# PSUM instead of SBUF for the operands of the small VectorE chain that orders the experts

## The chip, the cores and the metric

The kernel runs on one core of a Trainium2 chip. The metric is the device time of one execution in microseconds; the median of three executions of the kernel before is 777.16 us (775.65 to 778.07). One execution was also taken by the hardware profiler: it lasted 776.65 us, of which the span from the first to the last instruction is 774.9 us. "TensorE" is PE in the rows, with PEld for its weight loads; VectorE is DVE, ScalarE is ACT, GpSimd is POOL, SyncE is SP.

## The reference

Three stages follow each other: linear attention with random features, a top-1 mixture of experts, and a dense MLP.

```python
def phi(x):                                   # attention, per batch and head
    proj = np.einsum('bhsd,md->bhsm', x, omega)
    h = proj - np.sum(x * x, axis=-1, keepdims=True) / 2.0
    return np.exp(h - np.max(h, axis=-1, keepdims=True)) / np.sqrt(m)
num = phi(q_s) @ (phi(k_s).T @ v);  x = num / (den + 1e-06)

logits = x @ w_gate                           # mixture of experts, N = 2304 tokens, D = 512
expert_idx = np.argmax(logits, axis=1)
for e in range(8):                            # F = 1024
    out[mask_e] = gate_w[mask_e] * (relu(x[mask_e] @ w1[e]) @ w2[e])

h = x @ w_in                                  # MLP, d_ff = 2048
g = np.where(h >= 1, h, np.where(h <= -1, 0.0, (h + 1) ** 2 / 4))
return g @ w_out
```

## The kernel before

The attention stage writes the tokens' vectors `x` to a DRAM buffer `xd` and, beside that, finds each token's expert. An order of its instructions is made by a planner (class `Plan`); its tasks use eight PSUM buffers `ps` of 2 KB per partition, which come from a pool `psp` that is closed when the stage ends. The planner's last tasks count the tokens per expert and put the token numbers into lists (`slots`).

After the planner's tasks stands a chain written out by hand in program order (L1061 to L1122). One small TensorE product (L1080) adds up the tokens per expert into PSUM buffer 0. VectorE then copies the eight counts to SBUF (L1082), makes keys from them (L1083, L1084), compares the keys with each other (L1085), sums the comparisons into places (L1086), turns the places into an 8 by 8 one-hot table `hot` (L1088), and uses this table to reorder the counts, the expert numbers, the offsets and the lists (L1089 to L1104). With the offsets per expert, `offe`, L1115 and the six steps after it give each token its position in the ordered output. Every step is one VectorE instruction on at most 144 elements per partition.

Then the expert stage begins. Its tiles of tokens are gathered from `xd` by indirect DMAs that GpSimd issues (L1177), three for each expert. The first three are those of expert 0, whose list is ready before the chain (L935). Four new PSUM pools, `ps_x`, `ps_h`, `ps_y` and `ps_q` (L1158 to L1161, eight buffers of 2 KB per partition), take the room that `psp` had. The first work of the new stage on TensorE is `m_x0`: it runs 14 products whose result nobody reads, into a buffer of `ps_h`, then four transposes of the first gathered tile into buffers of `ps_x` and `ps_y`, then twice three idle products and four transposes:

```python
idle = ps_h.tile([P, 512], F32, name="ph", tag="ph")...          # L1206
for i, _ in rows(0):
    for _ in range((14, 3, 3)[i]):
        nc.tensor.matmul(idle, lhsT=oneb, rhs=oneb..., start=True, stop=True)   # L1209
    for d in range(4):
        m_turn(0, d, i, px[d])                                    # L1183
for d in range(4):
    m_split(0, d, px[d])                                          # L1189, L1190
```

ScalarE and VectorE split the transposed tiles in two parts (L1189, L1190), and TensorE's products of expert 0 follow (L1230 to L1232). The order on each engine is the order of the program, and each engine runs its instructions strictly in that order. A first write into a buffer of a new pool waits until the last instruction that uses the room of the closed pool is done. The offsets `offe` are read by L1115 through this statement, which the change leaves as it is:

```python
nc.vector.tensor_tensor(out=rr, in0=ohall, in1=offe.rearrange("p e o -> p o e").to_broadcast([P, NTILE, E]), op=ALU.mult)
```

Of the kernel before, what the change touches and what calls it, by code (L numbers as in the profile page):

```python
# [14 lines left out]
ALU = mybir.AluOpType  # L15
AX = mybir.AxisListType.X
# [3 lines left out]
P = 128  # L20
B, H, S, HD = 4, 8, 576, 64
NT, D, E, F, FF = 2304, 512, 8, 1024, 2048
NTILE = NT // P
WS = (288, 264, 272, 280, 288, 304, 328, 344)
W = max(WS)
NB = 3
# [10 lines left out]
C_TRI, C_IOTA, C_C8, C_WS, C_THR, C_TOK, C_ID, C_END = 0, 128, 512, 520, 528, 544, 580, 708  # L37
# [174 lines left out]
def kernel(  # L212
# [14 lines left out]
    nc = tc.nc  # L227
# [18 lines left out]
    oneb = cp.tile([P, P], BF16, name="oneb")  # L246
# [3 lines left out]
    rsb, ohall = seen[:, :, 0], seen[:, 0:NTILE, 1]  # L250
# [230 lines left out]
    with ExitStack() as actx:  # L481
# [4 lines left out]
        def ring(n, shape, name, dtype=F32, pool=ac):  # L486
            return [pool.tile(shape, dtype, name=f"{name}{i}") for i in range(n)]

        plan = Plan({
            "ps": ring(8, [P, 4, P], "ps", pool=psp),  # L490
            "blk": ring(7, [P, 2 * H, HD], "blk"),
            "sqt": ring(2, [P, 2 * H, HD], "sqt"),
            "th": ring(4, [P, 4, P], "th"),
            "pp": ring(11, [P, H, P], "pp"),
            "qt": ring(4, [P, 4, P], "qt"),
            "nx": ring(5, [P, H, HZ + 1], "nx"),
            "xr": ring(3, [P, H, HD], "xr"),
# [79 lines left out]
        dve, act, pool = nc.vector, nc.scalar, nc.gpsimd  # L577
# [434 lines left out]
        for s, u in enumerate(units):  # L1012
# [11 lines left out]
            if which == "k" and blk[0] != "s" and blk[1] == 1:  # L1024
                b = blk[0]
# [9 lines left out]
            for us, b0, b1 in new:  # L1035
                t = len(cts)
                kvs = [d for b in {b0, b1} for hf_ in range(2) for d in kvdone[b, hf_]]
                cts.append(c_tasks(t, us, kvs, s + 2 + 0.5 * len(new)))
                if t in groups:
                    t0, n = groups[t]  # L1040
                    prev_run = r_tasks(t0, cts[t0:t0 + n], s + 3.5, prev_run)
            if s >= 4 and s % 6 == 1 and wk < 4:
                key = wseq[wk]
# [5 lines left out]
            if s in (33, 35):  # L1049
                key = wseq[wk]  # L1050
# [10 lines left out]
        def small(name, shape):  # L1061
            return ap.tile(shape, F32, name=name, tag=name, bufs=1)

        def col(c, n):
            return cs[:, c:c + n]

        n, key, at_, nums, off, offe = [small(f"t{i}", [P, E, 1]) for i in range(6)]
        inc, ones, nv = [small(f"u{i}", [P, E]) for i in range(3)]
        hot, prod = small("hot", [P, E, E]), small("prod", [P, NB, E, E])
        g = prod[:, 0:2].rearrange("p m a b -> p (m a b)").rearrange("p (e j) -> p e j", j=16)  # L1070
        tot = small("ttot", [P, 1])

        def row(t):
            return t.rearrange("p a o -> p o a").to_broadcast([P, E, E])

        def flat(t):
            return t[:, :, 0]

        pn = plan.tiles["ps"][0][:, 0, :]
        nc.tensor.matmul(pn[:, 0:E], lhsT=oneb, rhs=rsb[:, NTILE, :], start=True, stop=True)  # L1080
        dve.memset(ones, 1.0)
        dve.tensor_copy(flat(n), pn[:, 0:E])  # L1082
        dve.scalar_tensor_tensor(out=flat(key), in0=flat(n), scalar=8.0, in1=col(C_C8, E), op0=ALU.mult, op1=ALU.add)  # L1083
        dve.memset(key[:, 0, :], 0.0)  # L1084
        dve.tensor_tensor(out=prod[:, 0], in0=row(key), in1=key.to_broadcast([P, E, E]), op=ALU.is_lt)  # L1085
        dve.reduce_sum(flat(at_), prod[:, 0], axis=AX)  # L1086
        iota = col(C_IOTA, E).rearrange("p (e o) -> p e o", o=1)
        dve.tensor_tensor(out=hot, in0=iota.to_broadcast([P, E, E]), in1=row(at_), op=ALU.is_equal)  # L1088
        dve.tensor_tensor(out=prod[:, 0], in0=hot, in1=row(n), op=ALU.mult)  # L1089
        dve.tensor_tensor(out=prod[:, 1], in0=hot, in1=row(iota), op=ALU.mult)  # L1090
        dve.reduce_sum(flat(nums), prod[:, 0], axis=AX)
        dve.reduce_sum(inc, prod[:, 1], axis=AX)
        dve.tensor_copy(ints[:, 4, :], inc)
        dve.tensor_tensor_scan(out=inc, data0=ones, data1=flat(nums), initial=0.0, op0=ALU.mult, op1=ALU.add)
        dve.tensor_sub(flat(off), inc, flat(nums))
        dve.tensor_copy(ints[:, 0, :], flat(off))
# [3 lines left out]
        for m in range(NB):  # L1100
            dve.reduce_sum(slots[:, m, :], prod[:, m], axis=AX)
        dve.tensor_copy(gidx[:, :, 1:E], slots[:, :, 1:E])
        dve.tensor_tensor(out=prod[:, 0], in0=hot.rearrange("p r e -> p e r"), in1=row(off), op=ALU.mult)
        dve.reduce_sum(flat(offe), prod[:, 0], axis=AX)  # L1104
        dve.tensor_sub(flat(n), flat(nums), col(C_WS, E))
        thr = col(C_THR, 16).rearrange("p (o j) -> p o j", o=1).to_broadcast([P, E, 16])
# [13 lines left out]
                                op0=ALU.logical_shift_right)  # L1120
# [495 lines left out]
    for qd in range(1, 4):  # L1616
        if qd == 3:
            z_fetch(2 * ORDER[0])
        for n, p in enumerate(ORDER):
# [11 lines left out]
            if (qd, n) == (3, 2):  # L1631
                flat = yp.tile([P, 3 * YW], F32, name="yF", tag="yT")
# [24 lines left out]
    with tc.If(tot > 0):  # L1657
# [3 lines left out]
        for e in range(E):  # L1661
# [4 lines left out]
            with tc.For_i(0, cnt_e, 1) as i:  # L1666
# [3 lines left out]
                for j in range(16):  # L1670
# [4 lines left out]
                    out=fx, out_offset=None, in_=xd,  # L1675
# [5 lines left out]
                for f in range(8):  # L1681
                    ph = ps_h2.tile([P, 512], F32, name="ph2", tag="ph2")[:, 0:P]
                    o = f % 2 * P
                    for d in range(4):
                        nc.tensor.matmul(ph, lhsT=fw[f // 2 * 4 + d][:, o:o + P],
                                         rhs=fxt[:, d * P:(d + 1) * P], start=(d == 0), stop=(d == 3))
                    nc.vector.tensor_scalar_max(fh[:, f, :], ph, 0.0)
                for j in range(16):
                    c, f = divmod(j, 8)
                    src = w2[ee, f * P:(f + 1) * P, c * 256:(c + 1) * 256]  # L1690
                    nc.sync.dma_start(out=fw[j], in_=src.rearrange("o p f -> p (o f)"))
                for d in range(4):
                    py = ps_h2.tile([P, 512], F32, name="ph2", tag="ph2")[:, 0:P]
                    o = d % 2 * P
                    for f in range(8):
                        nc.tensor.matmul(py, lhsT=fw[d // 2 * 8 + f][:, o:o + P], rhs=fh[:, f, :],
                                         start=(f == 0), stop=(f == 7))
                    nc.scalar.activation(fy[:, d, :], py, AF.Copy)
                po = ps_o.tile([P, D], F32, name="po", tag="po")
                for qd in range(4):  # L1700
# [3 lines left out]
                    for f in range(4):  # L1704
                        ph = ps_h2.tile([P, 512], F32, name="ph2", tag="ph2")[:, 0:P]
                        for d in range(4):
                            nc.tensor.matmul(ph, lhsT=fin[d][:, f * P:(f + 1) * P], rhs=fy[:, d, :],
                                             start=(d == 0), stop=(d == 3))
                        nc.vector.tensor_scalar(out=fg[:, f, :], in0=ph, scalar1=-1.0, scalar2=1.0,
                                                op0=ALU.max, op1=ALU.min)  # L1710
                        nc.scalar.activation(fg[:, f, :], fg[:, f, :], AF.Square, scale=0.5, bias=half)
                        nc.vector.tensor_tensor(out=fg[:, f, :], in0=ph, in1=fg[:, f, :], op=ALU.max)
                    for c in range(4):
# [3 lines left out]
                                         stop=(qd == 3 and c == 3))  # L1717
                nc.vector.tensor_copy(fo, po)
                nc.gpsimd.indirect_dma_start(
                    out=out, out_offset=bass.IndirectOffsetOnAxis(ap=fu, axis=0), in_=fo, in_offset=None)  # L1720
# [36 lines left out]
```

## Time and profile before

| | |
|---|---|
| median of three executions | 777.16 us (775.65 to 778.07) |
| profiled execution | 776.65 us, span 774.9 us |
| TensorE (PE) busy | 745.1 us, 96% of the span |
| PE weight loads (PEld) | 684.0 us, 88% |
| VectorE (DVE) busy | 515.7 us, 67% |
| ScalarE (ACT) busy | 436.7 us, 56% |
| GpSimd (POOL) busy | 376.6 us, 49% |
| mean granted TensorE clock | 0.991 |
| DMA | 164.25 MB, mean 212 GB/s |

A row of the timeline has the start in us from the beginning of the span, the duration in us, the engine, the line, the operation, the tiles by name and the shapes, and in square brackets how long the engine had been idle and what ended that. The chain that is changed lies between 151 and 158 us, at the border between the attention stage and the expert stage.

### The profile page before, as it was taken

The numbers are of one execution on the slowest core, as the hardware profiler recorded it, in microseconds if no ns is written. First come the engines' busy times: TensorE is split into PE (matmuls) and PEld (weight loads), VectorE is DVE, ScalarE is ACT, GpSimd is POOL, SyncE is SP. The second block draws the span as 40 slices with busy tenths as digits, with TensorE's granted clock in tenths as the row PEclk, the third lists the DMA queues.
The fourth block names the chain that finished last, engine by engine and source line by source line (L and its number), as shares of the span: only waits on it lengthen the run. The fifth ranks groups of instructions, "written<-read, shape, count | busy, mean of one in ns | idle before, by whom it ended". The sixth has DMA issues, their size and how long they took to land. (4 is left out here: it accounts for less than half of the span.)

```text
span 774.9 us, 17116 instructions
## 1 busy us (share of the span) xinstructions
PE 745.1 (96%) x6476; PEld 684.0 (88%) x6476; DVE 515.7 (67%) x1104; ACT 436.7 (56%) x1061; POOL 376.6 (49%) x429
## 2 busy tenths in 40 slices
PE   5799999699999999999999999899999999999997
PEld 4698899489999999999988889788998899889985
DVE  3688888965667567565686775876656766575553
ACT  5999999353322222222477766676577655763441
POOL 6665951645654564425548875323343143343212
PEclk9999999899999999999999999999999999999999
DMA  9949511356765765655537769798696996977822
GB/s 231 230 100 255 158 69 30 123 166 179 213 193 178 221 212 179 207 166 161 163 117 305 274 249 330 285 328 269 177 375 189 307 319 168 332 239 285 315 97 85
DMA packets 94236, 164.25 MB, mean 212 GB/s; under 512 B 28528, under 2 KB 61424, under 8 KB 94144
## 3 DMA queue, kind: packets, MB, share of 16 engines
q1 hardware_dynamic: 79680, 94.96, 39.2%
q0 software_dynamic: 14112, 67.44, 27.0%
q8 instruction: 53, 0.87, 0.4%
q10 hardware_dynamic: 352, 0.66, 0.3%
q14 instruction: 39, 0.32, 0.1%
HBM read 122.93 MB, written 40.11 MB: 210 GB/s over the span
## 5 line engine op out<-in xcount | busy, mean ns | idle before, releaser
L1433 PE MATMUL po<-wh,g 128*128 128x512 f32 x288 | 113.8, 395 | 0.7 <-ACT st L1439 0.7
L1435 PE MATMUL po<-wh,g 128*128 128x512 f32 x288 | 113.9, 395 | 0.0
L1434 PE MATMUL po<-wl,g 128*128 128x512 f32 x288 | 113.6, 395 | 0.0
L351 POOL TENSOR_TENSOR wl<-wz,wh 128x256 fp32r<-128x256 f32 (+1 forms) x43 | 40.5, 948 | 95.3 <-ACT wh L365 92.8
L674 ACT ACTIVATE pp<-ps,bi 128x128 f32<-128x128 f32 x288 | 84.4, 487 | 0.0
L329 POOL TENSOR_SCALAR wh<-wra 128x1024 fp32r<-128x1024 f32 x43 | 50.2, 1170 | 61.2 <-DMA wra<-in_moe_w_dram 26.9
L1248 PE MATMUL py<-hh,wh 128*128 128x288 f32 (+6 forms) x256 | 77.5, 303 | 0.0
L1230 PE MATMUL ph<-xh,wh 128*128 128x288 f32 (+6 forms) x256 | 76.7, 300 | 0.7 <-ACT xh L1189 0.4
L1231 PE MATMUL ph<-xl,wh 128*128 128x288 f32 (+6 forms) x256 | 76.6, 299 | 0.1
L1250 PE MATMUL py<-hh,wl 128*128 128x288 f32 (+6 forms) x256 | 76.6, 299 | 0.0
L1232 PE MATMUL ph<-xh,wl 128*128 128x288 f32 (+6 forms) x256 | 76.5, 299 | 0.0
L1249 PE MATMUL py<-hl,wh 128*128 128x288 f32 (+6 forms) x256 | 76.3, 298 | 0.0
L1395 DVE TENSOR_TENSOR g<-cl,g 128x384 fp32r<-128x384 f32 x78 | 47.0, 603 | 38.9 <-ACT g L1391 37.9
L1235 ACT ACTIVATE hh<-ph 128x288 fp32r<-128x288 f32 (+6 forms) x64 | 26.7, 418 | 70.2 <-PE ph L1232 69.1
L1435 PEld LDWEIGHTS po<-wh,g 128*128 128x128 f32 x288 | 54.2, 188 | 13.1 <-DVE g L1395 0.4
L1433 PEld LDWEIGHTS po<-wh,g 128*128 128x128 f32 x288 | 54.2, 188 | 12.4 <-ACT st L1439 1.0
L1434 PEld LDWEIGHTS po<-wl,g 128*128 128x128 f32 x288 | 54.2, 188 | 11.5
L1236 DVE SCALAR_TENSOR_TENSOR hl<-ph,hh 128x288 fp32r<-128x288 f32 (+6 forms) x64 | 29.3, 461 | 52.0 <-ACT hh L1235 51.7
L1391 ACT ACTIVATE g<-cl 128x384 fp32r<-128x384 f32 x78 | 40.5, 520 | 39.7 <-DVE cl L1390 38.4
L441 DVE TENSOR_TENSOR wl<-wra,wh 128x1024 fp32r<-128x1024 f32 x43 | 61.0, 1421 | 2.4 <-POOL wh L329 2.4
L1253 ACT ACTIVATE yT<-py 128x288 f32<-128x288 f32 (+7 forms) x32 | 13.4, 418 | 83.6 <-PE py L1250 80.5
L663 DVE TENSOR_REDUCE nsq<-ps 128x4 f32<-128x512 f32 x72 | 48.1, 683 | 8.1 <-PE ps L658 8.0
(226 smaller groups left out, 2149.8 us busy)
## 6 DMA issues: line engine op xcount, KB each, us to landing
yS<-yd POOLq DMA_DIRECT2D x32, 768.0 KB, 12.2
wra<-in_moe_w_dram SPq DMA_DIRECT2D x43, 512.0 KB, 4.1
ys<-yd POOLq DMA_DIRECT2D x25, 768.0 KB, 11.9
wraw<-in_moe_w_dram SPq DMA_DIRECT2D x20, 512.0 KB, 4.0
yd<-tt SPq DMA_DIRECT2D x24, 384.0 KB, 2.7
yd<-ys SPq DMA_DIRECT2D x9, 768.0 KB, 4.3
wra<-in_moe_w_in_dram SPq DMA_DIRECT2D x12, 512.0 KB, 5.4
wra<-in_moe_w_out_dram SPq DMA_DIRECT2D x11, 512.0 KB, 7.6
```

Source lines behind the costliest of these rows:

```text
L329: nc.gpsimd.tensor_scalar(out=hi, in0=t, scalar1=1.0, scalar2=1.0, op0=ALU.mult, op1=ALU.mult)
L441: nc.vector.tensor_sub(lo, t, hi.bitcast(F32))
L674: act.activation(at(ppb)[:, 2 * j + i, :], at(pjb[i])[:, j, :], AF.Exp, bias=r["bi"][:, j, i:i + 1])
L1230: nc.tensor.matmul(ph, lhsT=wh[:, d, c], rhs=xh, start=(d == 0), stop=False)
L1231: nc.tensor.matmul(ph, lhsT=wh[:, d, c], rhs=xl, start=False, stop=False)
L1232: nc.tensor.matmul(ph, lhsT=wl[:, d, c], rhs=xh, start=False, stop=(d == 3))
L1248: nc.tensor.matmul(py, lhsT=wh[:, a, c], rhs=hh, start=(f == 0), stop=False)
L1249: nc.tensor.matmul(py, lhsT=wh[:, a, c], rhs=hl, start=False, stop=False)
L1250: nc.tensor.matmul(py, lhsT=wl[:, a, c], rhs=hh, start=False, stop=(f == 7))
L1433: nc.tensor.matmul(po, lhsT=gh[:, c], rhs=wh, start=(f == 0), stop=False)
L1434: nc.tensor.matmul(po, lhsT=gh[:, c], rhs=wl, start=False, stop=False)
L1435: nc.tensor.matmul(po, lhsT=gl[:, c], rhs=wh, start=False, stop=(f == 3))
```

## The change

The counts stay in PSUM (`sums`), and the keys (`key`), the places (`at_`), the one-hot table (`hot`) and the offsets per expert (`offe`) are placed in PSUM buffer 0 of the old pool, `plan.tiles["ps"][0]`. The first key is set to zero by a multiplication instead of a memset, and the keys and the counts are copied to SBUF tiles (`keys`, `n`) for the steps that take them as the second input.

```diff
-        n, key, at_, nums, off, offe = [small(f"t{i}", [P, E, 1]) for i in range(6)]
+        pn = plan.tiles["ps"][0]
+        sums, key, at_ = [pn[:, 0, 16 * i:16 * i + E] for i in range(3)]
+        hot = pn[:, 1, 0:E * E].rearrange("p (a b) -> p a b", a=E)
+        nums, off, n, keys = [small(f"t{i}", [P, E, 1]) for i in range(4)]
+        offe = pn[:, 3, 0:E].rearrange("p (e o) -> p e o", o=1)
-        pn = plan.tiles["ps"][0][:, 0, :]
-        nc.tensor.matmul(pn[:, 0:E], lhsT=oneb, rhs=rsb[:, NTILE, :], start=True, stop=True)
-        dve.memset(ones, 1.0)
-        dve.tensor_copy(flat(n), pn[:, 0:E])
-        dve.scalar_tensor_tensor(out=flat(key), in0=flat(n), scalar=8.0, in1=col(C_C8, E), op0=ALU.mult, op1=ALU.add)
-        dve.memset(key[:, 0, :], 0.0)
-        dve.tensor_tensor(out=prod[:, 0], in0=row(key), in1=key.to_broadcast([P, E, E]), op=ALU.is_lt)
-        dve.reduce_sum(flat(at_), prod[:, 0], axis=AX)
-        dve.tensor_tensor(out=hot, in0=iota.to_broadcast([P, E, E]), in1=row(at_), op=ALU.is_equal)
+        nc.tensor.matmul(sums, lhsT=oneb, rhs=rsb[:, NTILE, :], start=True, stop=True)
+        dve.scalar_tensor_tensor(out=key, in0=sums, scalar=8.0, in1=col(C_C8, E), op0=ALU.mult, op1=ALU.add)
+        dve.tensor_scalar(out=key[:, 0:1], in0=key[:, 0:1], scalar1=0.0, scalar2=None, op0=ALU.mult)
+        dve.tensor_copy(flat(keys), key)
+        dve.tensor_copy(flat(n), sums)
+        dve.tensor_tensor(out=prod[:, 0], in0=line(key), in1=keys.to_broadcast([P, E, E]), op=ALU.is_lt)
+        dve.reduce_sum(at_, prod[:, 0], axis=AX)
+        dve.tensor_tensor(out=hot, in0=column(col(C_IOTA, E)), in1=line(at_), op=ALU.is_equal)
         ...
         dve.tensor_copy(ints[:, 4, :], inc)
+        dve.memset(ones, 1.0)
         dve.tensor_tensor_scan(out=inc, data0=ones, data1=flat(nums), initial=0.0, op0=ALU.mult, op1=ALU.add)
         ...
-        dve.tensor_tensor(out=prod[:, 0], in0=hot.rearrange("p r e -> p e r"), in1=row(off), op=ALU.mult)
+        dve.tensor_tensor(out=prod[:, 0], in0=hot.rearrange("p r e -> p e r"), in1=line(flat(off)),
+                          op=ALU.mult)
         dve.reduce_sum(flat(offe), prod[:, 0], axis=AX)
```

VectorE at the beginning of the chain, before (`ps0` is PSUM buffer 0 of the old pool, `t` and `u` are small SBUF tiles; the bracket names the engine whose signal is waited for):

```order
L1081 MEMSET u1_3063 128x8
L1082 COPY t0_3056<-ps0_134 128x8 [waits PE_49]
L1083 SCALAR_TENSOR_TENSOR t1_3057<-t0_3056,cs_95 128x8 [waits DVE_49]
L1084 MEMSET t1_3057 128x1 [waits DVE_49]
L1085 TENSOR_TENSOR prod_3066<-t1_3057 128x64 [waits DVE_49]
L1086 TENSOR_REDUCE t2_3058<-prod_3066 128x8 [waits DVE_49]
```

and VectorE at the same place in the changed kernel:

```order
L1087 SCALAR_TENSOR_TENSOR ps0_134<-ps0_134,cs_95 128x8 [waits PE_49]
L1088 TENSOR_SCALAR ps0_134<-ps0_134 128x1 [waits DVE_49]
L1089 COPY t3_3059<-ps0_134 128x8 [waits DVE_49]
L1090 COPY t2_3058<-ps0_134 128x8
L1091 TENSOR_TENSOR prod_3063<-ps0_134,t3_3059 128x64 [waits DVE_49]
L1092 TENSOR_REDUCE ps0_134<-prod_3063 128x8 [waits DVE_49]
```

The copy out of PSUM is no longer the first step, there is one instruction more ahead of the comparison, and the memset of the ones has moved further down, to stand ahead of the scan.

VectorE near the end of the chain, before (`trr` is written by L1115):

```order
L1103 TENSOR_TENSOR prod_3066<-hot_3065,t4_3060 128x64
L1104 TENSOR_REDUCE t5_3061<-prod_3066 128x8 [waits DVE_49]
L1105 TENSOR_TENSOR t0_3056<-t3_3059,cs_95 128x8
L1107 TENSOR_TENSOR prod_3066<-cs_95,t0_3056 128x128 [waits DVE_49]
L1111 CAST ints_109<-ttot_3067 128x1 [waits DVE_49]
L1115 TENSOR_TENSOR trr_3100<-seen_102,t5_3061 128x144
```

and in the changed kernel:

```order
L1109 TENSOR_TENSOR prod_3063<-ps0_134,t1_3057 128x64
L1111 TENSOR_REDUCE ps0_134<-prod_3063 128x8 [waits DVE_49]
L1112 TENSOR_TENSOR t2_3058<-t0_3056,cs_95 128x8
L1114 TENSOR_TENSOR prod_3063<-cs_95,t2_3058 128x128 [waits DVE_49]
L1118 CAST ints_109<-ttot_3064 128x1 [waits DVE_49]
L1122 TENSOR_TENSOR trr_3097<-seen_102,ps0_134 128x144
```

The instructions stand in the same order, but PSUM buffer 0 is now used until L1122, which is L1115 of the kernel before; before, its last use was L1082.

TensorE at the border of the two stages, before (`ob` and `oa` belong to the last list product, `ph` is the idle products' buffer):

```order
L926 MATMUL ps_136<-oa,ob 128x8
L1080 LDWEIGHTS oneb
L1080 MATMUL ps_134<-seen,oneb 128x8
L1209 LDWEIGHTS oneb [waits DVE_49]
L1209 MATMUL ph<-oneb 128x512 [waits Activation_49]
```

and in the changed kernel:

```order
L926 MATMUL ps_136<-oa,ob 128x8
L1086 LDWEIGHTS oneb
L1086 MATMUL ps_134<-seen,oneb 128x8
L1216 LDWEIGHTS oneb [waits DVE_49,PE_49]
L1216 MATMUL ph<-oneb 128x512 [waits Activation_49]
```

The order on TensorE is the same; at the first idle product a wait for TensorE's own count has been added, and the wait for VectorE stands in the same place. Which of VectorE's instructions fulfils it is not in these rows: in the program before it is L1082, in the changed one L1122. From L1086 on the changed kernel's lines are higher by 6 or 7, so that its L1190 is L1183 of before and its L1216 is L1209.

## Rows read from the trace of the kernel before

**Rows 1.** The page, share of the span by engine:

```profile
PE 745.1 (96%) x6476; PEld 684.0 (88%) x6476; DVE 515.7 (67%) x1104; ACT 436.7 (56%) x1061; POOL 376.6 (49%) x429
```

**Rows 2.** Busy time by stretch: stretch, length, engines, granted clock, DMA share, GB/s:

```profile
159.10:200.00 40.90, 40.55 (x312) 39.91 (x313) 27.01 (x40) 19.61 (x44) 18.78 (x16) 1.00 0.57 173
200.00:250.00 50.00, 50.00 (x414) 49.90 (x414) 31.25 (x42) 11.74 (x31) 28.58 (x22) 1.00 0.66 201
```

**Rows 3.** What TensorE waited for from 159 us to the end:

```profile
PE ph L1540 <- DMA yS<-yd: 1.7, 2, 1.2
PE po L1433 <- ACT st L1439: 0.7, 1, 0.7
PE ph L1405 <- POOL ys L1152: 0.7, 1, 0.7
PE ph L1540 <- ACT tt L1550: 0.5, 1, 0.5
```

**Rows 4.** Timeline of TensorE, 150 to 160 us:

```profile
151.32 4.50 PE L1209 MATMUL ph<-oneb 128*128 128x512 bf16 x14 [0.53 <-DVE t L1082]
155.69 0.41 PE L1183 MATMUL px<-ident,xg 128*128 128x128 f32 x2
...
156.16 0.81 PE L1209 MATMUL ph<-oneb 128*128 128x512 bf16 x3
157.03 0.44 PE L1183 MATMUL px<-ident,xg 128*128 128x128 f32 x2
...
157.52 0.81 PE L1209 MATMUL ph<-oneb 128*128 128x512 bf16 x3
158.26 0.31 PE L1183 MATMUL px<-ident,xg 32*128 32x32 f32 x2
...
159.13 0.40 PE L1230 MATMUL ph<-xh,wh 128*128 128x288 f32 x1 [0.44 <-ACT xh L1189]
```

**Rows 5.** Timeline of VectorE, 149 to 160 us:

```profile
151.11 0.15 DVE L1082 COPY t<-ps 128x8 f32<-128x8 f32 x1
...
151.63 0.22 DVE L1085 TENSOR_TENSOR prod<-t 128x64 f32<-128x64 f32 x1
...
152.40 0.22 DVE L1089 TENSOR_TENSOR prod<-hot,t 128x64 f32<-128x64 f32 x1
...
153.46 0.17 DVE L1095 TENSOR_TENSOR t<-u,t 128x8 f32<-128x8 f32 x1
153.66 0.17 DVE L1096 CAST ints<-t 128x8 int32<-128x8 f32 x1
153.74 0.16 DVE L1097 CAST ints<-t 128x8 int32<-128x8 f32 x1
...
156.41 0.30 DVE L1115 TENSOR_TENSOR trr<-seen,t 128x144 f32<-128x144 bf16 x1
```

**Rows 6.** Timeline of all engines, VectorE just ahead of the chain:

```profile
148.78 0.16 DVE L901 TENSOR_TENSOR rpr<-ps,seen 128x16 f32<-128x16 f32 x1
...
149.06 0.17 DVE L906 TENSOR_REDUCE ps<-rpr 128x2 f32<-128x16 f32 x1
...
149.27 1.02 DVE L918 TENSOR_TENSOR ob<-cs,ps 128x384 bf16<-128x384 f32 x2
```

**Rows 7.** Timeline of GpSimd, 150 to 175 us:

```profile
151.93 1.18 POOL L1177 DMA_INDIRECT xg<-xd,gidx  x1 [2.92 <-DVE prod L1085]
...
158.38 0.95 POOL L1177 DMA_INDIRECT xg<-xd,gidx  x1 [0.31 <-PE ph L1209]
```

**Rows 8.** The idle products' line: count, duration in ns (min/median/max):

```profile
L1209 PE MATMUL ph<-oneb x20: 379/380/635, 151.3 to 158.0; 128*128 128x512 bf16 x20
```

**Rows 9.** Busy time by short stretches, columns as in rows 2:

```profile
150.90:151.30 0.40, 0.00 (x0) 0.00 (x0) 0.33 (x4) 0.00 (x0) 0.00 (x0) 0.50 0.00 0
...
153.50:154.00 0.50, 0.50 (x3) 0.22 (x2) 0.47 (x5) 0.00 (x0) 0.50 (x1) 0.50 0.44 82
154.00:154.50 0.50, 0.50 (x4) 0.20 (x3) 0.50 (x6) 0.00 (x0) 0.38 (x1) 1.00 0.65 180
```

More of the change, by code (lines that the diff above doesn't have):

```diff
@@ L1065, in col @@
             return cs[:, c:c + n]
-        n, key, at_, nums, off, offe = [small(f"t{i}", [P, E, 1]) for i in range(6)]
+        pn = plan.tiles["ps"][0]
[3 more added lines that the diff above has]
+        offe = pn[:, 3, 0:E].rearrange("p (e o) -> p e o", o=1)
         inc, ones, nv = [small(f"u{i}", [P, E]) for i in range(3)]
-        hot, prod = small("hot", [P, E, E]), small("prod", [P, NB, E, E])
+        prod = small("prod", [P, NB, E, E])
@@ L1070, with column, line @@
         g = prod[:, 0:2].rearrange("p m a b -> p (m a b)").rearrange("p (e j) -> p e j", j=16)
         tot = small("ttot", [P, 1])
-        def row(t):
-            return t.rearrange("p a o -> p o a").to_broadcast([P, E, E])
+        def column(t):
+            return t.rearrange("p (e o) -> p e o", o=1).to_broadcast([P, E, E])
+        def line(t):
+            return t.rearrange("p (o e) -> p o e", o=1).to_broadcast([P, E, E])
         def flat(t):
             return t[:, :, 0]
-        pn = plan.tiles["ps"][0][:, 0, :]
@@ L1080 @@
-        nc.tensor.matmul(pn[:, 0:E], lhsT=oneb, rhs=rsb[:, NTILE, :], start=True, stop=True)
-        dve.memset(ones, 1.0)
-        dve.tensor_copy(flat(n), pn[:, 0:E])
-        dve.scalar_tensor_tensor(out=flat(key), in0=flat(n), scalar=8.0, in1=col(C_C8, E), op0=ALU.mult, op1=ALU.add)
-        dve.memset(key[:, 0, :], 0.0)
-        dve.tensor_tensor(out=prod[:, 0], in0=row(key), in1=key.to_broadcast([P, E, E]), op=ALU.is_lt)
-        dve.reduce_sum(flat(at_), prod[:, 0], axis=AX)
-        iota = col(C_IOTA, E).rearrange("p (e o) -> p e o", o=1)
@@ L1088 @@
-        dve.tensor_tensor(out=hot, in0=iota.to_broadcast([P, E, E]), in1=row(at_), op=ALU.is_equal)
-        dve.tensor_tensor(out=prod[:, 0], in0=hot, in1=row(n), op=ALU.mult)
-        dve.tensor_tensor(out=prod[:, 1], in0=hot, in1=row(iota), op=ALU.mult)
+        nc.tensor.matmul(sums, lhsT=oneb, rhs=rsb[:, NTILE, :], start=True, stop=True)
+        dve.scalar_tensor_tensor(out=key, in0=sums, scalar=8.0, in1=col(C_C8, E), op0=ALU.mult, op1=ALU.add)
+        dve.tensor_scalar(out=key[:, 0:1], in0=key[:, 0:1], scalar1=0.0, scalar2=None, op0=ALU.mult)
@@ new lines @@
+        dve.tensor_copy(flat(keys), key)
[3 more added lines that the diff above has]
+        dve.tensor_tensor(out=hot, in0=column(col(C_IOTA, E)), in1=line(at_), op=ALU.is_equal)
+        dve.tensor_tensor(out=prod[:, 0], in0=hot, in1=line(flat(n)), op=ALU.mult)
+        dve.tensor_tensor(out=prod[:, 1], in0=hot, in1=line(col(C_IOTA, E)), op=ALU.mult)
```

## The prediction

> **What bounds the kernel.** I read the shares by engine first: TensorE is busy for 745.1 of 774.9 us [rows 1]. The busy time by stretch says where: from 159.1 us, when the expert stage's products begin, TensorE is busy for 40.55 of 40.90 us and then for 50.00 of 50.00 [rows 2]. The table of its waits from there to the end holds 1.7 + 0.7 + 0.7 + 0.5 = 3.6 us beside the 0.44 us ahead of the first product [rows 3, 4]. So after 159 us the kernel is a row of products with almost no gaps, and whatever sets the moment at which that row begins, sets the end. The chain that the change touches lies just ahead of this moment, so I read the border, 150 to 160 us, engine by engine.
>
> TensorE's part of the border [rows 4]: 14 idle products from 151.32, four transposes from 155.69, three idle products from 156.16, four transposes from 157.03, three idle products, four transposes from 158.26, and the first real product at 159.13. The first idle product was released by L1082, VectorE's copy of the counts, which ends at 151.11 + 0.15 = 151.26 [rows 5]; 0.06 us later TensorE starts. It is the last instruction on VectorE that touches the old PSUM pool, and the idle products write into the room of that pool. Everything after it on TensorE is queued behind it. The rest of VectorE's chain runs beside the idle products and the gathers; nobody on the path waits for it before 159 us.
>
> **The change, part by part.**
>
> *The release of the old PSUM room.* With the changed kernel the last use of PSUM buffer 0 is no longer the copy at 151.26 but L1122, the product with `offe`, which is L1115 of before. The idle products' wait is counted up to that instruction. In the trace of before L1115 starts at 156.41 and takes 0.30, so it ends at 156.71 [rows 5]. The release moves by 156.71 - 151.26 = 5.45 us. This is the large term. The 14 idle products, the 12 transposes and the 6 other idle products all stand behind it in TensorE's queue, so they can't be done meanwhile, though the gathered tiles lie ready. ScalarE's first split gets the same wait, but it needs the transposes anyway.
>
> *The chain's own length up to that instruction.* Before, the comparison L1085 starts 0.52 us after the copy L1082 [rows 5]. In the changed kernel three dependent steps stand there: the keys, the zeroing and the copy of the keys. A dependent step follows its predecessor after 0.20 us (L1095 at 153.46, L1096 at 153.66), so the comparison starts about 0.60 us after the first step: +0.08. The second copy doesn't depend on the first; such a step follows after 0.08 us (L1096 to L1097) and lies in the shadow of the 0.20. The memset of the ones moves down to a place where, before, the scan waited for the step ahead; two pitches of about 0.1 stand for one of 0.2: nothing. I take +0.1.
>
> *Operands in PSUM instead of SBUF.* About twelve instructions up to the release read or write PSUM that did not before. Rows with PSUM: the copy L1082 takes 0.15 against 0.17 for the cast L1096 out of SBUF; L901, two inputs of which one is PSUM, takes 0.16 against 0.17 for L1095 with both in SBUF; L906, which writes PSUM, takes 0.17, and L918, which reads what it wrote, starts at 149.27, 0.04 after its end [rows 5, 6]. So the bounds are 12 times -0.02 and 12 times +0.02, -0.24 to +0.24, and I take 0. [...]
>
> *Two SBUF inputs no longer.* What the change takes away is the second SBUF input of these steps. If that input held up VectorE or GpSimd here, rows would show it. L1085 takes 0.22 before GpSimd's first gather starts at 151.93, and L1089, of the same size, takes 0.22 at 152.40, in the middle of it [rows 5, 7]. GpSimd's first gather instruction takes 1.18, the last, after the chain is over, 0.95 [rows 7]. At most the first gather is shorter by 1.18 - 0.95 = 0.23. This is worth nothing once TensorE starts its transposes 5 us later than the data lie there. It ranges from 0 to -0.23 on the gathers and 0 on the path.
>
> *What is given back.* Before, TensorE waited a little for the gathers inside the border. One idle product takes 0.38 and three in a row take 0.81, so they are (0.81 - 0.38) / 2 = 0.21 us apart [rows 4, 8]. The second four transposes could have started at 156.16 + 3 x 0.213 = 156.80 and started at 157.03; the third could have at 157.52 + 0.64 = 158.16 and started at 158.26 [rows 4]. These 0.23 + 0.10 = 0.33 us fall away, as all gathers have landed by then. The first four started right behind the 14 idle products.
>
> *The clock.* [...] If all 14 ran slow, that would be 7 x 0.213 = +1.5 us; if none did, -1.5.
>
> *Sum.* 5.45 + 0.1 - 0.33 = 5.2 us later at the first real product (159.13 becomes about 164.3). From there the row of products is full, and its feeders (weights on SyncE's queue, splits on GpSimd) are not behind this wait, so they are early rather than late; what depends on the products moves with them. The profiled execution would go from 776.65 to 781.9 (span 774.9 to 780.1). It lies 0.5 under the median of the three runs, 777.16, which gives 782.4. I take 782.1, between the two.
>
> **The rivals.**
>
> *The clock stays low longer.* TensorE now stands quite still for 6 us ahead of the idle products, where it had rested 0.53 us [rows 4]. If the slow stretch then covers all 14 idle products: 5.2 + 1.5 = 6.7, so 783.6. For it: the longer rest. Against it: at 150.9 the clock was already at the lower of its two levels [rows 9].
>
> *The delay is caught up later.* TensorE's 3.6 us of later waits [rows 3] would be the places for it, if what it waited for there came at a fixed moment: loads of `yd` (1.7), the rest splits and additions on ScalarE and GpSimd (1.9). Then only 5.2 - 3.6 = 1.6 us are left, 778.7, which is within 0.3%. Against it: those transfers and splits work on results of the same products and move with them. It decides from 2.9 us of regained waits on.
>
> *TensorE isn't held.* If the idle products were released as before, by the first step that reads the sums, the border would be set by the gathers, as at 157.03. A relief of the first gather by 0.23 would then make it at most 0.33 us shorter: 776.8, not slower. The place is the first idle product, and the point is whether its wait is for the first or for the last step on PSUM buffer 0. For it: the wait stands at the same place and on the same engine as before. Against it: the rule by which L1082 released it in the trace, the last user of the old room, names L1122 in the changed kernel, and the program's counts say so too.
>
> **How the numbers follow.** I give the forecast 0.81, the longer slow clock 0.09, the caught-up delay 0.06 and the missing hold 0.04. The forecast's own uncertainty: the clock's share of 1.5 either way, though mostly under 0.7, PSUM 0.24, the chain 0.1 to 0.3, and about 1 us from the median of a few runs (the three shown spread over 2.4). So 779.7 to 784.5, which also takes in the first rival; the two others, 0.10, are left out with the tails. A measurement of this kernel can tell about 0.3%, 2.3 us, from no change. Slower than that, above 779.5, are the forecast, save its lowest tail, and the first rival: 0.89. No change: the two other rivals and that tail, 0.10. Faster: 0.01, for which no row gives a mechanism of 2.3 us.
>
> **What would show it.** In the changed kernel's timeline of TensorE the first idle product should start near 156.9 instead of 151.3, with about 6 us of idle time ahead of it ended by L1122, and the first real product near 164.3. The chain on VectorE should end within 0.4 us of where it ended before, and the gathers should start as before. About half of the 14 idle products should be slow. The stretch from the first real product to the end should be as long as before, within 1 us. The prediction is wrong if the idle products start before 152, if the later waits of TensorE go from 3.6 us to nearly none, or if the chain's steps on PSUM are clearly shorter or longer than those on SBUF.

## The result, and the profile after

The changed kernel takes 784.06 us (median of 5, 781.34 to 785.69) against 776.51 for the kernel before (median of 5). The two medians lie 7.6 us apart; the ratio of the times, by which I go from here on, is 1.0081 with a 95% interval of 1.0060 to 1.0101, about 6.3 us (4.7 to 7.8) slower. In two later sessions the ratio was 1.0037 (1.0024 to 1.0051) and 1.0061 (1.0038 to 1.0083). The profiled execution took 784.61 us, span 782.8.

The timeline of TensorE in the changed kernel, at the border; the first row is the product of the counts, and L1216, L1190 and L1237 are L1209, L1183 and L1230 of [rows 4]:

```profile
152.21 0.17 PE L1086 MATMUL ps<-seen,oneb 128*128 128x8 bf16 x1
...
158.48 5.89 PE L1216 MATMUL ph<-oneb 128*128 128x512 bf16 x14 [6.10 <-DVE trr L1122]
...
164.21 0.38 PE L1190 MATMUL px<-ident,xg 128*128 128x128 f32 x2
...
165.29 0.38 PE L1190 MATMUL px<-ident,xg 128*128 128x128 f32 x2
...
165.73 0.81 PE L1216 MATMUL ph<-oneb 128*128 128x512 bf16 x3
166.47 0.31 PE L1190 MATMUL px<-ident,xg 32*128 32x32 f32 x2
...
167.34 0.40 PE L1237 MATMUL ph<-xh,wh 128*128 128x288 f32 x1 [0.44 <-ACT xh L1196]
```

and the product of the counts in the kernel before, which [rows 4] leave out:

```profile
150.63 0.17 PE L1080 MATMUL ps<-seen,oneb 128*128 128x8 bf16 x1
```

The attention stage ended 1.58 us later in this execution. The end of that stage moves by up to 3.6 us between profiles of kernels that don't differ there (the product of the counts starts at 148.59 to 152.21), so I count from the start of the product of the counts. The stretch from there to the start of the first real product is called the border. It is 167.34 - 152.21 = 15.13 us, before 159.13 - 150.63 = 8.50. The border is 6.6 us longer. The bracket at the first idle product says by what: TensorE rested for 6.10 us and was released by L1122.

VectorE's timeline in the changed kernel:

```profile
152.68 0.17 DVE L1087 SCALAR_TENSOR_TENSOR ps<-ps,cs 128x8 f32<-128x8 f32 x1
152.88 0.17 DVE L1088 TENSOR_SCALAR ps<-ps 128x1 f32<-128x1 f32 x1
153.08 0.17 DVE L1089 COPY t<-ps 128x8 f32<-128x8 f32 x1
...
153.28 0.22 DVE L1091 TENSOR_TENSOR prod<-ps,t 128x64 f32<-128x64 f32 x1
...
154.06 0.22 DVE L1094 TENSOR_TENSOR prod<-ps,t 128x64 f32<-128x64 f32 x1
...
156.49 0.21 DVE L1109 TENSOR_TENSOR prod<-ps,t 128x64 f32<-128x64 f32 x1
...
158.04 0.29 DVE L1122 TENSOR_TENSOR trr<-seen,ps 128x144 f32<-128x144 bf16 x1
```

The chain hardly got longer or shorter by its operands. From its first step to the end of the product with `offe` it takes 158.33 - 152.68 = 5.65 us, and 5.60 before [rows 5]. L1091 and L1094 with PSUM operands take the 0.22 of L1085 and L1089 in SBUF. One step got shorter: L1109, the product of the turned table with the offsets, takes 0.21 and took 0.25 in the kernel before, where the table lies in SBUF:

```profile
154.81 0.25 DVE L1103 TENSOR_TENSOR prod<-hot,t 128x64 f32<-128x64 f32 x1
```

Of the runs further below, it is 0.25 in the two kernels "offe alone in PSUM" and "table and offe in SBUF", which have the table in SBUF, and 0.21 in the two with the table in PSUM, "idle products in old room" and "changed, no first idle products". Whether that is the second SBUF input or the way in which this step reads the table, by its columns, no run shows; it is worth 0.04 us.

GpSimd's first and last gather instruction of the border, as in [rows 7]:

```profile
153.51 1.18 POOL L1184 DMA_INDIRECT xg<-xd,gidx  x1 [2.92 <-DVE prod L1091]
...
159.95 0.95 POOL L1184 DMA_INDIRECT xg<-xd,gidx  x1 [0.30 <-DVE spos L1129]
```

Their durations are those of before to the hundredth, 1.18 and 0.95 us [rows 7]. The gathers were not relieved by taking the second SBUF input away: the first took 1.18 us beside both kinds of chain, and the last one runs after the chain.

The granted clock (the third figure from the end) around the end of the idle products, and the first stretch of real products:

```profile
163.40:163.90 0.50, 0.50 (x2) 0.15 (x1) 0.00 (x0) 0.00 (x0) 0.00 (x0) 0.50 0.02 8
163.90:164.40 0.50, 0.50 (x4) 0.34 (x3) 0.00 (x0) 0.00 (x0) 0.00 (x0) 0.91 0.00 0
...
167.30:208.20 40.90, 40.68 (x313) 40.10 (x314) 26.86 (x40) 19.80 (x45) 16.02 (x13) 1.00 0.51 161
```

The granted clock was 0.50 until 164.0, which is about the last of the 14 idle products; the way from the first of them to the first transpose is 164.21 - 158.48 = 5.73 us, before 155.69 - 151.32 = 4.37 [rows 4, 9]. From the first real product on nothing changed: 782.8 - 167.34 = 615.5 us to the end, before 774.9 - 159.13 = 615.8. So of the 7.9 us by which the two spans differ, 1.6 lie ahead of the border, 6.6 in it and -0.3 behind it. The later waits of TensorE are those of [rows 3], with 1.8 for 1.7:

```profile
PE ph L1547 <- DMA yS<-yd: 1.8, 1, 1.8
PE ph L1412 <- POOL ys L1159: 0.7, 1, 0.7
PE po L1440 <- ACT st L1446: 0.7, 1, 0.7
PE ph L1547 <- ACT tt L1557: 0.5, 1, 0.5
```

### The profile page after: what moved, and what is told of

It is laid out like the page before. It is cut to its first block, busy times and chain, and to the rows that moved or that the text cites. A ratio compares the mean times of both kernels' runs of the same rounds, so it can differ in the third digit from the quotient of the medians.

```text
span 782.8 us, 17118 instructions
## 1 busy us (share of the span) xinstructions
PE 744.8 (95%) x6476; PEld 683.3 (87%) x6476; DVE 517.2 (66%) x1105; ACT 436.6 (56%) x1061; POOL 378.9 (48%) x429
## 5 line engine op out<-in xcount | busy, mean ns | idle before, releaser
L1237 PE MATMUL ph<-xh,wh 128*128 128x288 f32 (+6 forms) x256 | 76.6, 299 | 0.5 <-ACT xh L1196 0.4
```

Source lines behind the costliest of these rows:

```text
L1237: nc.tensor.matmul(ph, lhsT=wh[:, d, c], rhs=xh, start=(d == 0), stop=False)
```

## The experiments

The theory (A): the loss is the hold of the old PSUM room, which sits on TensorE's path, and what the clock adds to it. The rival (B): the steps on PSUM, or the stage ahead, cost the time. All figures of the first three columns count from the start of the product of the counts, in us, each from one profile; the third is the border. The ratio is to the kernel before in the same session.

| kernel | first idle product | first transpose | first real product | ratio of times (95%) |
|---|---|---|---|---|
| before | 0.69 | 5.06 | 8.50 | |
| before, again | 0.70 | 5.77 | 8.91 | 1.0009 (0.9991 to 1.0026) |
| changed | 6.27 | 12.00 | 15.13 | 1.0081 (1.0060 to 1.0101) |
| changed, second session | 6.27 | 11.88 | 15.01 | 1.0037 (1.0024 to 1.0051) |
| changed, third session | 6.27 | 11.20 | 14.34 | 1.0061 (1.0038 to 1.0083) |
| offe alone in PSUM | 6.23 | 10.86 | 13.99 | 1.0059 (1.0037 to 1.0080) |
| changed, offe in SBUF | 4.63 | 9.05 | 12.18 | 1.0019 (0.9999 to 1.0040) |
| changed, table and offe in SBUF | 1.97 | 6.28 | 9.41 | 1.0011 (0.9997 to 1.0025) |
| changed, idle products in old room | 0.03 | 6.33 | 9.49 | 0.9996 (0.9982 to 1.0010) |
| changed, both cures | 0.03 | 5.15 | 10.49 | 1.0014 (0.9999 to 1.0029) |
| changed, both cures, again | 0.03 | 6.15 | 9.31 | 1.0002 (0.9986 to 1.0019) |
| changed, no first idle products | none | 6.33 | 11.70 | 1.0034 (1.0016 to 1.0052) |
| before, no first idle products | none | 5.06 | 10.42 | 0.9995 (0.9984 to 1.0006) |

The session in which the changed kernel ran a second time also held the runs of "offe in SBUF", the first "both cures" and "before, no first idle products".

**Idle products in the old room.** The whole chain stays in PSUM; only the 14 idle products are moved ahead of the pools' change.

```diff
         nc.tensor.matmul(sums, lhsT=oneb, rhs=rsb[:, NTILE, :], start=True, stop=True)
+        for _ in range(14):
+            nc.tensor.matmul(plan.tiles["ps"][7], lhsT=oneb, rhs=..., start=True, stop=True)
...
-                for _ in range((14, 3, 3)[i]):
+                for _ in range((0, 3, 3)[i]):
```

> The changed kernel with the 14 idle products of TensorE moved to before the border: they follow the product of the counts and write into buffer 7 of the old PSUM pool, so they need not wait for the release; the transposes still do. Theory A (the loss is the later release of the old PSUM room, 5.5 us, plus 1.5 us of slow clock): the idle products start about 0.5 us earlier than in the kernel before and warm the clock while the chain runs, and the transposes start at the release, 1.1 us later than in the kernel before. With 0.33 us of waits given back that is +0.8 us on the kernel before: 776.9 to 777.9, the loss almost gone although the whole chain is still on PSUM. Rival B (the steps on PSUM themselves, or the stage ahead of them, cost the time): as the changed kernel, 782 to 785.

TensorE's timeline of this kernel:

```profile
149.46 0.17 PE L1086 MATMUL ps<-seen,oneb 128*128 128x8 bf16 x1
149.49 5.98 PE L1088 MATMUL ps<-oneb 128*128 128x512 bf16 x14
155.79 0.41 PE L1193 MATMUL px<-ident,xg 128*128 128x128 f32 x2 [0.32 <-PE ps L1088]
...
158.95 0.40 PE L1240 MATMUL ph<-xh,wh 128*128 128x288 f32 x1 [0.44 <-ACT xh L1199]
```

and VectorE's last use of the old room in it:

```profile
155.29 0.29 DVE L1125 TENSOR_TENSOR trr<-seen,ps 128x144 f32<-128x144 bf16 x1
```

The idle products lie beside the chain. They and the chain end almost together, at 155.47 and 155.58, and the transposes start at 155.79; the bracket names the idle products, and which of the two ended the wait isn't decided by these rows. The border is 9.49, 1.0 longer than in the first profile of the kernel before, and the time 777.23 against 778.12: no loss that can be measured. The chain with all its PSUM steps costs nothing measurable (0.9996, 0.9982 to 1.0010) once the 14 idle products don't queue behind it. Rival B falls.

**offe alone in PSUM.** The kernel before, with one tile moved:

```diff
-        n, key, at_, nums, off, offe = [small(f"t{i}", [P, E, 1]) for i in range(6)]
+        n, key, at_, nums, off = [small(f"t{i}", [P, E, 1]) for i in range(5)]
+        offe = plan.tiles["ps"][0][:, 3, 0:E].rearrange("p (e o) -> p e o", o=1)
```

> The kernel before with one edit: the offsets per expert, offe, are placed in PSUM buffer 0 of the old pool; keys, places and one-hot table stay in SBUF. Only two VectorE instructions touch PSUM that did not before. Theory A: the last use of the old room moves as far as in the whole change, so the time is that of the changed kernel, +6 to +7.5 us on the kernel before: 782.5 to 784. Rival B: two steps out of some twelve, so at most a sixth of the loss, 776.5 to 777.8.

TensorE's timeline:

```profile
150.46 0.17 PE L1081 MATMUL ps<-seen,oneb 128*128 128x8 bf16 x1
156.69 4.79 PE L1210 MATMUL ph<-oneb 128*128 128x512 bf16 x14 [6.06 <-DVE trr L1116]
...
164.45 0.40 PE L1231 MATMUL ph<-xh,wh 128*128 128x288 f32 x1 [0.44 <-ACT xh L1190]
```

781.94 us, +0.59%, 4.6 us (2.9 to 6.2). The middle of that is under the +6 to +7.5 that I had expected. The way from the first idle product to the first transpose was 4.63 us, against 5.73 in the first profile of the changed kernel; the granted clock was 0.50 for 3.3 us of it, there for 5.5. But it is more than three times the 1.3 us that rival B allows at most. One late reader of the old room is enough for the loss.

**Table and offe in SBUF**, and **offe alone in SBUF**: the changed kernel with its last uses of the old room taken away, from the back.

```diff
-        hot = pn[:, 1, 0:E * E].rearrange("p (a b) -> p a b", a=E)
+        hot = small("hot", [P, E, E])            # first of the two kernels only
-        offe = pn[:, 3, 0:E].rearrange("p (e o) -> p e o", o=1)
+        offe = small("t5", [P, E, 1])
```

> The changed kernel with the one-hot table and offe back in SBUF; counts, keys and places stay in PSUM. The last use of the old room is then the step that writes the table, which in the kernel before ended 1.1 us after the copy of the counts. Theory A: the idle products start 1.1 us later than in the kernel before after a rest of about 1.6 us, 0.33 us come back, so +0.8 us with the slow clock lasting 2.7 us as before (776.9 to 777.9), and up to +2.3 us if the longer rest prolongs it too. Rival B: half of the steps on PSUM remain, so about half of the loss, 779.5 to 781.

> The changed kernel with offe alone back in SBUF; the one-hot table stays in PSUM, so the last use of the old room is the product of the table with the offsets, which starts 4.28 us and ends 4.49 us after the product of the counts in the changed kernel's trace, where the whole change has 6.12. Theory A (the release sets the loss): the first real product 3.5 us later than in the kernel before, counted from the product of the counts, plus 0 to 1.5 us by when the clock rises: +3.5 to +5 us on the time, between the run with the table in SBUF and the whole change. Rival B (the steps on PSUM cost the time): one step less than the whole change, so nearly its loss, +5.5 to +6.5 us.

The first, then the second kernel's first idle products, with what released them:

```profile
152.22 4.47 PE L1216 MATMUL ph<-oneb 128*128 128x512 bf16 x14 [1.79 <-DVE hot L1093]
```

```profile
153.22 4.58 PE L1216 MATMUL ph<-oneb 128*128 128x512 bf16 x14 [4.46 <-DVE prod L1109]
```

The release follows the last user of the room, step by step: 1.97, 4.63 and 6.27 us after the product of the counts, and the border is 9.41, 12.18 and 15.13. The times are in the same order, 1.0011, 1.0019 and (same session as the second) 1.0037, though the first is from another session and its interval overlaps with that of the second. The second is below the +3.5 to +5 us that its border makes one expect; 1.5 us (-0.1 to 3.1) was measured. That session is taken up below.

**No first idle products**, in the changed kernel and in the kernel before:

```diff
-                for _ in range((14, 3, 3)[i]):
+                for _ in range((0, 3, 3)[i]):
```

> The changed kernel without its 14 first idle products (they compute nothing that is read). Theory A with the slow clock: the transposes start right at the release, about 6 us earlier than in the changed kernel, but they and the six other idle products run at the lower clock and the first real products partly too; I expect the first real product some 5 us after the release instead of 8.9 and a clock that rises about 5.5 us after TensorE starts: 3 to 4 us faster than the changed kernel, 779 to 780.5, still slower than the kernel before. Rival: if the idle products were needed to bring the clock up and the real products run slow for long without them, no gain or a loss against the changed kernel, 783 or more.

> The kernel before without its 14 first idle products (they compute nothing that is read). There the transposes wait for the gathers, so nothing starts earlier; what goes is only the warming of the clock. Transposes, the six other idle products and the first real products run at the lower clock: in the changed kernel without the 14 the way from the first transpose to the first real product took 5.4 us against 3.4 at full clock, and the clock rose 9.3 us after the first transpose. Expected +2 us at the first real product and up to +2 more behind it: +2 to +4 us on the kernel before. If the slow clock is over sooner, +1 to +2; if the idle products are worth nothing, 0.

The timeline of TensorE in the changed kernel without them, and after it in the kernel before without them:

```profile
155.47 0.66 PE L1190 MATMUL px<-ident,xg 128*128 128x128 f32 x2 [6.17 <-DVE trr L1122]
...
160.84 0.61 PE L1237 MATMUL ph<-xh,wh 128*128 128x288 f32 x1 [0.31 <-ACT xh L1196]
```

```profile
156.39 0.66 PE L1183 MATMUL px<-ident,xg 128*128 128x128 f32 x2 [4.88 <-DMA xg<-xd,gidx]
...
161.75 0.40 PE L1230 MATMUL ph<-xh,wh 128*128 128x288 f32 x1 [0.38 <-ACT xh L1189]
```

In the changed kernel the transposes then start at the release, and the border falls from 15.13 to 11.70 us although a transposing pair takes 0.66 instead of 0.38 us and the first real products run at a granted clock of 0.50 until about 164.8. At +0.34% it has lost 2.6 us (1.2 to 4.0). That is clearly less than the changed kernel in its first session (6.3), but not clearly less than in its third (4.7) or than "offe alone" in the same session (4.6), whose intervals overlap with it. Its profile shows more than that: the border is 2.8 to 3.2 us longer than in the two profiles of the kernel before, and the way from the first real product to the end is 618.2 us instead of 615.8.

In the kernel before without the 14, the transposes start when the first gather lands, 5.06 us after the product of the counts. With the 14 they start right behind them, which was at 5.06 us in the first profile and, with a later rise of the clock (4.2 us after the first idle product instead of 2.7), at 5.77 in the second. I expected a loss of 2 us and more, and the border is 1.5 to 1.9 us longer, but the time is the same (0.9984 to 1.0006). The expectation was missed.

**Both cures**: the idle products in the old room, and table and offe in SBUF, run twice.

> The changed kernel with both cures: the 14 idle products in buffer 7 of the old pool, right after the product of the counts, and the one-hot table and offe in SBUF, so that the transposes' wait ends early too; counts, keys and places are still in PSUM. Theory A: the border is again set by the gathers, as in the kernel before: within 0.5 us of it. If fewer steps with two SBUF inputs helped the gathers or the chain, this is where it would show, as up to 0.5 us less. Rival B: half of the steps on PSUM remain, so some 2 to 3 us more than the kernel before.

> Changed kernel with idle products in the old room and with table and offe in SBUF, a second time: its first profile had ScalarE's first split 2.1 us late for a reason that its rows don't give, and the clock fell once more behind that. If this was one execution's accident, the border is 8.3 to 8.8 us and the time within 0.1% of the kernel before; if it belongs to this kernel, 10.5 us again and +0.1 to +0.3%.

In the first profile ScalarE's first split started 2.1 us after the transposes it needs had ended (at 159.0):

```profile
161.14 0.41 ACT L1199 ACTIVATE xh<-px 128x288 fp32r<-128x288 f32 x1 [12.83 <-remote]
```

While TensorE waited for it, the granted clock fell to 0.50 at 160.8, and it rose again at 167.6; the way from the first real product to the end was 618.8 us, instead of 615.5 to 616.3 in the other kernels that have their first idle products. In the second profile the split followed at once, and the time was that of the kernel before (1.0002). Its border, 9.31, is longer than the 8.3 to 8.8 that I had expected: its idle products ran at a granted clock of 0.50 for 5.8 us, and the transposes stood right behind them. What held ScalarE in the first is not in its rows; it didn't come again. By its time the first run was 1.1 us (-0.1 to 2.3) over the kernel before, where I had expected at most 0.5. No version was faster than the kernel before by more than the measurement can tell.

**The changed kernel and the kernel before, again.**

> The changed kernel once more, beside its variants on the same chip. Theory A with the clock: +5.1 us when the slow clock covers half of the idle products and up to +6.6 when it covers all of them, so +5 to +6.6 us, and in its profile the distance from the product of the counts to the first real product is 13.6 to 15.2 us against 8.5 in the kernel before. If the +6.6 of the first profile is the rule, the distance is 15.1 again.

> The kernel before once more, with a profile from the same chip as the changed kernel's. The changed kernel's loss was 0.81% in one session and 0.37% in another, while the way from the product of the counts to the first real product was 15.1 and 15.0 us in its two profiles. Theory 1: the kernel before has a border that is not always 8.5 us; gathers that land later, or a later clock, prolong it in some executions up to 10.5 (as in the two kernels with an early release that were profiled in that session), and behind a late release the same delays are hidden. Then this profile shows 8.5 to 10.5 us, and the loss is the smaller the longer it is. Theory 2: the border is always 8.5 us and the difference lies in the attention stage ahead, whose end moved by 3 us from profile to profile (product of the counts at 148.6 to 152.2). The time is within 0.2% of the kernel before either way.

> The changed kernel a third time, beside the kernel before on one chip. Both theories: +0.4 to +0.9%; in the profile 13.6 to 15.2 us from the product of the counts to the first real product, by how many of the 14 idle products run at the lower clock.

The kernel before has a border of 8.91 us in its second profile, the changed one 15.01 and 14.34. Of the kernel before, second profile:

```profile
149.57 5.24 PE L1209 MATMUL ph<-oneb 128*128 128x512 bf16 x14 [0.53 <-DVE t L1082]
154.64 0.38 PE L1183 MATMUL px<-ident,xg 128*128 128x128 f32 x2
```

In the second profile of the changed kernel the bracket at the first idle product names L1117 instead of L1122:

```profile
156.57 0.15 DVE L1117 TENSOR_REDUCE ttot<-u 128x1 f32<-128x8 f32 x1
...
156.82 0.29 DVE L1122 TENSOR_TENSOR trr<-seen,ps 128x144 f32<-128x144 bf16 x1
```

The idle product starts at 157.26 there, 0.15 us after the end of L1122, as in the first profile (158.48 and 158.33), and 0.54 after that of L1117; so I read it as the same release.

So the difference of the borders is 5.4 to 6.6 us, and two of three sessions measure 4.7 and 6.3 us. The second session measures 2.9 us (1.9 to 4.0), where I had expected 5 to 6.6; there the kernel before took 779.3 us, 1 to 3 us more than in the other sessions, while the changed kernel took 782.44, within its usual range. So in that session the kernel before lost time that the changed one did not. That fits a longer border of the kernel before, and would explain the missed expectation of the kernel without idle products too, but no profile of the kernel before was taken on that chip. It would not explain why the changed kernel without its first idle products, from another session, measured less than its profile shows as well. The profile of the kernel before from the third session can't decide it, since the loss was a usual one there. This stays open.

## Why the prediction was right

The time lay in the range (784.06 in 779.7 to 784.5), near its upper end, and slower as forecast; the forecast value, 782.1, was 2 us low. The forecast loss, 5.2 us, lies between the 2.9 and the 6.3 us of the three sessions. Step by step:

*The release.* Forecast 5.45 + 0.1 us; in the traces the first idle product starts 6.27 instead of 0.69 us after the product of the counts, 5.58. It was released by L1122, as forecast, and it moved with the last user in the runs that have another one. The rival that TensorE isn't held is refuted.

*The chain.* Forecast +0.1 with ±0.24 for PSUM; measured 5.65 against 5.60 us.

*Two SBUF inputs.* Forecast 0 on the path and 0 to -0.23 on the gathers; measured 0 on the gathers, 1.18 and 0.95 us as before, and on the path 0.04 us less in the one step L1109, 0.21 for 0.25.

*Given back.* Forecast 0.33 us: from the first transpose to the first real product it was 159.13 - 155.69 = 3.44 us before [rows 4] and is 167.34 - 164.21 = 3.13 now. But it was 3.14 in the second profile of the kernel before, where TensorE didn't wait for a gather in the border, so this term is not there in every execution. And its smaller part was misread: the third transposes start 166.47 - 165.73 = 0.74 us after the idle products ahead of them in the changed kernel too, as 158.26 - 157.52 before, so those 0.10 us were no wait for the gathers.

*The clock.* This is the mis-sized term. I took 0, a rise 2.7 us after the first idle product as before, and gave +1.5 us, the rival with the slow clock, a chance of 0.09. The 1.5 us is an estimate: before, the granted clock was 0.50 for the first 2.7 us of the 14 and 1.00 from 154.0 on [rows 4, 9]; in those 2.7 us they stand 0.43 us apart (weight loads of L1209 at 152.15, 152.58 and 153.00), so six or seven fit in, and if the other seven stood 0.43 us apart too, instead of the 0.21 of [rows 4, 8], that would be 7 x 0.21 = 1.5 us more. In the three profiles of the changed kernel the way from the first idle product to the first transpose was 5.73, 5.61 and 4.93 us against 4.37: +1.4, +1.2 and +0.6. The first profile is accounted for: 5.58 + 1.36 - 0.31 = 6.6 us, which is the rival's 6.7 and not the forecast's 5.2. Against the 5.07 of the second profile of the kernel before, though, it is +0.7, +0.5 and -0.1, so how much of this term belongs to the change is not shown. The rival's reason, the long rest, is not borne out either (last section). The range held because it took in this rival.

*Caught up later.* Refuted: the later waits of TensorE are the same, and so is the way from the first real product to the end.

## What to carry to other kernels

Before a tile is moved into a pool that is about to be closed, ask what the next stage writes into that room: the last reader of the tile becomes a wait of the next stage, and one late reader cost here 4.6 us, about as much as the whole change with its 2.9 to 6.3. In this border TensorE's order mattered more than the length of the chain of small steps: with the idle products ahead of the wait the loss could not be measured any more (0.9996), although the chain took the same 5.65 us (149.93 to 155.58). Look for a gain where a row shows the cost: the rows named in the prediction put no cost on a second SBUF input (L1085 and L1089 take 0.22 us, without and with a gather beside them), and what the change took off VectorE's rows was 0.04 us in one step.

## What was not expected of the hardware

TensorE's granted clock, at 0.50 when the idle products start, rose to 1.00 after very different times in kernels that issue the same 14 products back to back: 2.7 and 4.2 us in the kernel before, after a rest of 0.53 us; 5.5, 5.3 and 3.9 in the changed one, after a rest of 6.1; 3.3 with offe alone in PSUM, after 6.06; 2.9 and 2.7 with offe, and with table and offe, in SBUF, after 4.46 and 1.79; 5.7, 2.8 and 5.8 where they follow the product of the counts at once (idle products in the old room, both cures twice). The rest ahead of them doesn't order these numbers. With transposes and real products in place of the 14 it rose about 9.4 us after the first transpose in the changed kernel and 4.8 in the kernel before. What a wait costs in clock can so be told only to about 1.5 us here.
